# Two queues for the first loads of a gated attention and feed-forward mix, and new orders for its five engines

## The chip, the cores and the metric

The kernel runs on one core of one Trainium2 chip. The metric is the device time of one execution in microseconds (us); lower is better. A core has five engines that run their own instruction streams and meet through semaphores: TensorE (matrix products; PE in the profile, and PEld for its weight loads), VectorE (DVE), ScalarE (ACT), GpSimd (POOL) and SyncE (SP), which here only issues transfers. Matrix products read SBUF and write PSUM, which has 8 banks of 128 x 512 floats. SyncE and ScalarE can each issue transfers (DMAs) on a queue of its own; the profile calls these queues SPq and ACTq.

## The reference

```python
def _A_ref(x, wqkv, w_phi, wo):          # x: 1 x 2048 x 512, 32 heads of 16
    q, k, v = split(x @ wqkv)
    pq = einsum("bhsd,hdf->bhsf", q, w_phi)
    pk = einsum("bhsd,hdf->bhsf", k, w_phi)
    phi_q = concatenate([softmax(pq), softmax(-pq)])
    phi_k = concatenate([softmax(pk), softmax(-pk)])
    kv = einsum("bhsf,bhsd->bhfd", phi_k, v)
    z = einsum("bhsf->bhf", phi_k)
    num = einsum("bhqf,bhfd->bhqd", phi_q, kv)
    den = einsum("bhqf,bhf->bhq", phi_q, z)[..., None] + 1e-6
    return merge_heads(num / den) @ wo
def _B_ref(x, w1, w2):                   # w1: 512 x 1376, w2: 1376 x 512
    return maximum(x @ w1, 0) @ w2
g = sigmoid((x * gate_w).sum(-1, keepdims=True))
out = g * _A_ref(...) + (1 - g) * _B_ref(...)
```

Inputs and output are bf16.

## The kernel before

The 2048 rows of x form 16 tiles of 128 rows (m = 0 to 15), and 4 chunks of 512 rows (c = 0 to 3). Most products want x transposed, in SBUF tile XT. Chunks 1 to 3 are transposed by the transfer that loads them (tasks x1, x2, x3). The first four tiles are loaded as they are, into a free slot of FT, and turned on TensorE by a product with the identity IDN: tasks xt0a to xt3b (line 321), two 128-column matmuls each, tile m in halves a and b. ScalarE copies half a of a turned tile out of PSUM (xe00, xe10, xe20, xe30; line 333), VectorE half b (xe01 to xe31; line 335). The table XB says which PSUM banks each turned tile uses; with XB = (0,1), (6,7), (0,1), (6,7), tile 2 has to wait until tile 0 was copied out of banks 0 and 1.

The program is a set of small named tasks, each with its engine and the tasks that it depends on. A table ORDER holds, for each engine, the order in which its tasks are emitted; the waits are placed from the dependencies. Every engine does its tasks strictly in that order. The numbers `dur` and `lat` in the code are notes of the planner that made the orders; nothing emitted depends on them.

The tasks that matter below:

- warm0 (line 251): eight products of constants on TensorE, which keep it at work while the first load is under way; 3,456 columns in all.
- xa, wva, xb, wvb, w1a, wphi, wkT (lines 264 and 268): the first loads, all on SyncE's queue in this order. xa has tiles 0 to 2 of x (384 KB, three rows in each partition), xb tile 3 (128 KB), wva and wvb the two halves of the value weights (256 KB each), w1a 512 columns of w1 (512 KB); wkT is a transposing load of the key weights.
- v0a, v0b, ... v3a, v3b (line 369): the value product of tiles 0 to 3 in two halves, of two matmuls each; half a needs xe{m}0 and wva, half b xe{m}1 and wvb. ve0 to ve3 copy the results out on ScalarE (line 374). v4 to v15 are whole.
- h{c}_{k} (line 392), rl{c}_{k} (line 410): the first feed-forward layer, four matmuls a task, and its relu on ScalarE. The last 96 columns of the layer and the gate are hr{c} (line 400) and rr{c} (line 415), with a transposing transfer ht{c} (line 421).
- f1_j (line 351): folds w_phi into the key weights; fe1_j (lines 313, 315) copies the result out. It needs wkT and the block-diagonal w_phi (wbd, line 305).
- jobs k0 to k8 and q0 to q8, one or two tiles each: pr (line 449) projects, ev (line 482) copies out on ScalarE, mx and mn (lines 486, 488) are maximum and minimum on VectorE, t1 and t2 (line 495) the two subtractions on GpSimd, ex (line 500) the exponential on ScalarE, sm and rc (lines 502, 506) the sums and their reciprocals on VectorE, nm (lines 509 and 532) the division on GpSimd. For k, kv (line 516) sums key features times values over all tiles in PSUM; for q, ra (line 528) prepares the factor, tq{m} (line 535) transposes the features by a transfer on SyncE's queue, nd{m}_0 and nd{m}_1 (line 559) are numerator and denominator, rd and o (lines 565, 567) divide, and to{m} (line 572) transposes the result, again on SyncE's queue.
- b{m} (line 580, 11 matmuls) is the second feed-forward layer, a{m} (line 586, 4 matmuls) the output projection added in the same bank, oe{m} (line 631) the eviction on ScalarE, st{m} (line 634) the store, issued by ScalarE. Tile 15 is done in two column parts (lines 601, 612), so that its two stores go out from ScalarE and SyncE.
- ones (line 242): a memset on GpSimd that writes the column of ones into VS, from which z comes.

Of the kernel before, what the change touches and what calls it, by code (L numbers as in the profile page):

```python
# [15 lines left out]

ORDER = {
    "sp": (
        "xa wva xb wvb w1a wphi wkT w1b x1 gw w1c wqT x2 x3 w2a ht0 w2b ht1 wo ht3 tq0 tq1 tq3 tq2 to0 to1 tq4 "
        "tq5 to2 to3 tq6 tq7 to4 ht2 to5 tq9 tq8 to6 to7 tq10 tq11 to8 to9 tq12 tq13 to10 to11 tq14 tq15 to12 "  # L20
        "to13 to14 to15 st15_1 "
    ),
    "pool": (
# [5 lines left out]
    ),  # L29
    "act": (  # L30
# [8 lines left out]
    ),  # L39
    "dve": (  # L40
# [10 lines left out]
    ),  # L51
# [10 lines left out]
    ),  # L62
}

# [16 lines left out]
class _Graph:  # L81
# [6 lines left out]
    def add(self, name, eng, fn, deps=(), dur=0.1, lat=None, dma=False):  # L88
        assert name not in self.tasks, name
        found = []  # L90
        for d in deps:
            if d is None:
                continue
            t = self.tasks[d]
            if t not in found:
                found.append(t)
        self.tasks[name] = _Task(name, eng, fn, found, dur, self.LAT[eng] if lat is None else lat, dma)
        return name
# [44 lines left out]
def bass_gated_mix__linear_kernel_hedgehog__dense_activation_relu__prompt_kernel(  # L143
# [11 lines left out]
    x2 = A_x.rearrange("b s d -> (b s) d")  # L155
    o2 = out.rearrange("b s d -> (b s) d")
    S, D = x2.shape
# [23 lines left out]
    with ExitStack() as es:  # L181
# [67 lines left out]
        def pe_warm(q, sizes):  # L249
            for n in sizes:  # L250
                last = q.matmul(PS[:, 5, 0:n], ONE[:, 0:P], ONE[:, 0:n], start=True, stop=True)  # L251
            return last

        add("warm0", "pe", lambda q: pe_warm(q, (D, D, D, D, D, D, P, 2 * P)), (), dur=1.46)

        queue = {}

# [5 lines left out]
        def load(name, eng, out_, in_, deps=(), dur=0.1, lat=6.0, **how):  # L263
            add(name, eng, lambda q: q.dma_start(out=out_, in_=in_, **how), deps, dur=dur, lat=lat, dma=True)
            after_last(name, eng)
# [7 lines left out]

        w1r = B_w1.rearrange("(j p) n -> p j n", p=P)
        wvr = A_wqkv[:, 2 * D:3 * D].rearrange("(j p) n -> p j n", p=P)
        load("xa", "sp", FT[:, NF - 2, 0:3 * D], x2[0:3 * P, :].rearrange("(p t) d -> p (t d)", t=3), dur=0.47, lat=2.6)
        load("wva", "sp", WV[:, 0:2, :], wvr[:, 0:2, :], dur=0.47, lat=3.3)
        load("xb", "sp", FT[:, NF - 2, 3 * D:4 * D], x2[3 * P:4 * P, :], dur=0.47, lat=4.2)
        load("wvb", "sp", WV[:, 2:4, :], wvr[:, 2:4, :], dur=0.49, lat=3.8)
        load("w1a", "sp", W1[:, :, 0:512], w1r[:, :, 0:512], dur=0.5, lat=4.9)  # L280
        load("wphi", "sp", WPS[:, :, :], A_w_phi.rearrange("(g hl) r c -> (hl r) g c", g=ND), dur=0.55, lat=4.7)
        load_t("wkT", WT[:, ND:2 * ND, :], A_wqkv[:, D:2 * D], (), 4.55, 2.0)
# [31 lines left out]
            else:  # L314
                add(name, eng, lambda q: q.tensor_copy(out_, PS[:, b, :]), deps, dur=0.69)

        XB, FB = ((0, 1), (6, 7), (0, 1), (6, 7)), (6, 7, 0, 1)

        def pe_xt(q, m, n):
            for j in (2 * n, 2 * n + 1):  # L320
# [4 lines left out]
        for m in range(4):  # L325
            for n in range(2):
                add(f"xt{m}{'ab'[n]}", "pe", lambda q, m=m, n=n: pe_xt(q, m, n),
                    ("xa" if m < 3 else "xb", "ident", f"xe{m - 2}{n}" if m > 1 else None), dur=0.11)
            for n, eng in enumerate(("act", "dve")):
                xo = XT[:, 2 * n:2 * n + 2, m * P:(m + 1) * P]  # L330
                xi = PS[:, XB[m][n], 0:2 * P].rearrange("p (j t) -> p j t", j=2)
                if eng == "act":
                    add(f"xe{m}{n}", eng, lambda q, o=xo, i=xi: q.activation(o, i, ACT.Copy), (f"xt{m}a",), dur=0.38)
                else:
                    add(f"xe{m}{n}", eng, lambda q, o=xo, i=xi: q.tensor_copy(o, i), (f"xt{m}b",), dur=0.42)
# [6 lines left out]
        HB = (3, 4, 5)  # L342

        def rows(m):
            if m < 3:
                return o2[0:3 * P, :].rearrange("(p t) d -> p t d", t=3)[:, m, :]
            return o2[m * P:(m + 1) * P, :]

        def pe_fold(q, s, j, b):
            for i in range(ND):  # L350
                last = q.matmul(PS[:, b, i * P:(i + 1) * P], WT[:, s * ND + i, j * P:(j + 1) * P], WBD[:, i, :],  # L351
                                start=True, stop=True)
            return last

        for j in range(ND):
            b = FB[j]
            add(f"f1_{j}", "pe", lambda q, j=j, b=b: pe_fold(q, 1, j, b), ("wkT", *wbd, f"xe{3 - j // 2}{j % 2}"), dur=0.24)
            evict(f"fe1_{j}", ("dve", "act")[j % 2], WP[:, 1, j, :], b, (f"f1_{j}",))
        units = []
        for c in range(NC):  # L360
# [17 lines left out]
        for m in range(4):  # L378
            for n, js in enumerate(((0, 1), (2, 3))):
                add(f"v{m}{'ab'[n]}", "pe", lambda q, m=m, js=js: pe_v(q, m, js, VB[m]),  # L380
                    (f"xe{m}{n}", f"wv{'ab'[n]}", *((f"v{m}a",) if n else ())), dur=0.44)
            evict_v(m, VB[m], (f"v{m}b",))
        freed = {b: (f"ve{m}",) for m, b in enumerate(VB)}
        add("gt", "pe", lambda q: q.matmul(PS[:, 2, 0:ND], GWR[:, :], IDN[:, 0:ND], start=True, stop=True),
# [297 lines left out]
```

## Time and profile before

| | us |
|---|---|
| median of 3 runs | 150.82 (150.82 to 150.91) |
| the profiled execution | 150.61 |
| its span, first to last instruction | 148.8 |

| engine | busy us | share of the span |
|---|---|---|
| PE | 145.4 | 98% |
| DVE | 110.9 | 75% |
| POOL | 109.7 | 74% |
| ACT | 91.8 | 62% |
| PEld | 73.1 | 49% |

A row of the timeline has the start, the length, the engine, the line of the kernel, the operation and its operands (out<-in), the count (x) where like instructions are merged, and in brackets how long the engine had been idle and what ended that. Rows of the waits give the engine and what it waited for, then the total, the times and the longest. In the chain that ended last, each row is a start, a length and the work that the end of the execution hung on at that time. Matmuls are pipelined: a 512-column one is shown 379 ns long, while four of them take 0.86 us.

### The profile page before, as it was taken

To read this page: it belongs to the slowest core of one execution; us is meant where nothing else is said; L and a number is where in the kernel's file an instruction comes from. 1 tells how busy PE (TensorE), PEld (TensorE's weight loads), DVE (VectorE), ACT (ScalarE), POOL (GpSimd) and SP (SyncE) were. 2 spreads that over 40 slices of the span, in tenths; PEclk is the share of its full clock that TensorE was granted. 3 is DMA by queue.
4 is the path that set the end of the run, shared out by engine and by line. 5 is a ranking of instruction groups with operands and counts; after the bars stand their busy time and mean duration, and the time that the engine had idled before them with its cause. 6 is when DMAs were issued, how large, how long until landed. Compare 5 with 4: busy or idle time off the path is not lost.

```text
span 148.8 us, 2554 instructions
## 1 busy us (share of the span) xinstructions
PE 145.4 (98%) x984; PEld 73.1 (49%) x984; DVE 110.9 (75%) x169; ACT 91.8 (62%) x127; POOL 109.7 (74%) x73
## 2 busy tenths in 40 slices
PE   7999999999999999999999999999999999999994
PEld 2454444445446644455455544454545445445453
DVE  0345799999997769893979979799899966618301
ACT  3367779996795987865988691656545651303051
POOL 4000899999999999999999999999999924510000
PEclk9999999999999999999999999999999999999999
DMA  4999999300200500000000135964737587874543
GB/s 164 289 224 185 261 206 289 109 0 0 66 0 0 154 31 0 0 0 0 4 2 0 35 87 127 108 152 95 181 71 176 151 206 142 162 160 116 127 141 110
DMA packets 45524, 16.11 MB, mean 108 GB/s; under 512 B 39272, under 2 KB 45384, under 8 KB 45512
## 3 DMA queue, kind: packets, MB, share of 16 engines
q1 hardware_dynamic: 43208, 13.89, 42.9%
q10 hardware_dynamic: 2304, 2.06, 4.3%
q8 instruction: 8, 0.13, 0.4%
q14 instruction: 4, 0.03, 0.1%
HBM read 4.41 MB, written 2.10 MB: 44 GB/s over the span
## 4 chain that ended last, share of the span: by engine, by line
POOL 46%; PE 42%; issue 5%; DMA 3%; DVE 1%; SPq 1%; ACT 1%
POOL TS L495 25%; PE PS L580 19%; POOL FT L509 18%; PE PS L586 9%; DMA PHQ<-FT 3%; POOL FT L532 3%; PE PS L559 3%; PE PS L369 2%; PE PS L251 2%; PE PS L449 2%; PE PS L392 2%; PE PS L601 2%; SPq L535 1%; PE PS L321 1%; PE PS L351 1%
## 5 line engine op out<-in xcount | busy, mean ns | idle before, releaser
L495 POOL TENSOR_TENSOR TS<-MN,PB 128x1024 bf16<-128x1024 bf16 (+1 forms) x18 | 31.0, 1733 | 12.9 <-DVE MN L488 12.9
L392 PE MATMUL PS<-XT,W 128*128 128x512 bf16 x160 | 38.4, 379 | 0.0
L502 DVE TENSOR_REDUCE ZB<-FT 128x128 f32<-128x2048 bf16 (+1 forms) x18 | 36.4, 2029 | 1.9 <-ACT FT L500 1.8
L580 PE MATMUL PS<-W,HT 128*128 128x512 bf16 (+1 forms) x165 | 37.8, 379 | 0.0
L500 ACT ACTIVATE FT<-TS 128x2048 bf16<-128x2048 bf16 (+1 forms) x18 | 30.9, 1719 | 4.3 <-POOL TS L495 3.6
L495 POOL TENSOR_TENSOR TS<-PB,MX 128x1024 bf16<-128x1024 bf16 (+1 forms) x18 | 31.1, 1732 | 0.0
L449 PE MATMUL PS<-WP,XT 128*128 128x512 bf16 x128 | 30.1, 379 | 0.0
L509 POOL TENSOR_TENSOR FT<-FT,SC 128x2048 bf16<-128x2048 bf16 (+1 forms) x9 | 29.7, 3308 | 0.0
L631 ACT ACTIVATE OSB<-PS,OMG 128x512 bf16<-128x512 f32 x15 | 10.3, 686 | 24.9 <-PE PS L586 24.8
L410 ACT ACTIVATE HT<-PS 128x512 bf16<-128x512 f32 x40 | 22.6, 596 | 4.7 <-PE PS L392 3.9
L580 PEld LDWEIGHTS PS<-W,HT 128*128 128x128 bf16 (+1 forms) x165 | 15.4, 98 | 17.2 <-ACT OSB L631 0.7
L482 ACT ACTIVATE PB<-PS 128x1024 bf16<-128x1024 f32 (+1 forms) x18 | 16.7, 928 | 10.7 <-PE PS L449 5.7
L392 PEld LDWEIGHTS PS<-XT,W 128*128 128x128 bf16 x160 | 14.7, 98 | 16.4 <-ACT HT L410 0.9
L488 DVE TENSOR_REDUCE MN<-PB 128x64 bf16<-128x1024 bf16 (+1 forms) x18 | 19.4, 1090 | 4.4 <-ACT PB L482 4.3
L486 DVE TENSOR_REDUCE MX<-PB 128x64 bf16<-128x1024 bf16 (+1 forms) x18 | 19.4, 1086 | 3.6 <-ACT PB L482 3.6
L449 PEld LDWEIGHTS PS<-WP,XT 128*128 128x128 bf16 x128 | 12.2, 98 | 14.2 <-ACT PB L482 0.5
L369 PE MATMUL PS<-WV,XT 128*128 128x512 bf16 x64 | 16.4, 379 | 0.1
L532 POOL TENSOR_TENSOR FT<-FT,SR 128x1024 bf16<-128x1024 bf16 (+1 forms) x9 | 15.7, 1740 | 0.6
L586 PE MATMUL PS<-WO,OT 128*128 128x512 bf16 x60 | 14.8, 378 | 0.0
L567 DVE SCALAR_TENSOR_TENSOR OTM<-PS,EG,RD 128x256 bf16<-128x256 f32 x32 | 14.3, 468 | 0.2
L565 DVE RECIPROCAL RD<-PS 128x16 f32<-128x16 f32 x32 | 6.7, 235 | 9.0 <-PE PS L559 9.0
L374 ACT ACTIVATE VS<-PS 128x512 bf16<-128x512 f32 x16 | 9.4, 600 | 2.2 <-PE PS L369 2.2
(54 smaller groups left out, 97.5 us busy)
## 6 DMA issues: line engine op xcount, KB each, us to landing
out_dram<-OSB ACTq DMA_DIRECT2D x15, 128.0 KB, 2.0
W<-in_B_w_dram SPq DMA_DIRECT2D x1, 1280.0 KB, 7.4
W<-in_B_w_dram SPq DMA_DIRECT2D x2, 512.0 KB, 4.9
WV<-in_A_wqkv_dram SPq DMA_DIRECT2D x2, 256.0 KB, 3.7
WO<-in_A_wo_dram SPq DMA_DIRECT2D x1, 512.0 KB, 3.8
FT<-in_A_x_dram SPq DMA_DIRECT2D x1, 384.0 KB, 3.0
W<-in_B_w_dram SPq DMA_DIRECT2D x1, 352.0 KB, 3.6
PHQ<-FT SPq DMA_TRANSPOSE x16, 2.8
```

What stands on the lines that cost most here:

```text
L392: last = q.matmul(PS[:, b, :], W1[:, j, k * P:(k + 1) * P], XT[:, j, chunk(c)], start=(j == 0), stop=(j == ND - 1))
L410: add(f"rl{a}_{k}", "act", lambda q, a=a, k=k, b=b: q.activation(HT[:, k, chunk(a)], PS[:, b, :], ACT.Relu), (f"h{a}_{k}",), dur=0.6)
L449: last = q.matmul(PS[:, pj + n, :], XT[:, j, m * P:(m + 1) * P], WP[:, s, j, :], start=(j == 2), stop=(j == 1))
L486: add(f"mx_{J}", "dve", lambda q, sl=sl, w=w, i=pbg: q.tensor_reduce(MX[:, sl, 0:w * H], i, AX.X, ALU.max), (f"ev_{J}", old("t1")), dur=0. ...
L488: add(f"mn_{J}", "dve", lambda q, sl=sl, w=w, i=pbg: q.tensor_reduce(MN[:, sl, 0:w * H], i, AX.X, ALU.min), (f"ev_{J}", old("t2")), dur=0. ...
L495: add(f"{tn}_{J}", "pool", lambda q, o3=o3, a3=a3, b3=b3: q.tensor_tensor(o3, a3, b3, ALU.subtract), (f"{'mx' if sg == 0 else 'mn'}_{J}", ...
L500: add(f"ex_{J}", "act", lambda q, fs=fs, ts=ts, w=w: q.activation(FT[:, fs, 0:w * F], TS[:, ts, 0:w * F], ACT.Exp), (f"t1_{J}", f"t2_{J}", ...
L502: add(f"sm_{J}", "dve", lambda q, fs=fs, sl=sl, w=w: q.tensor_reduce(ZB[:, sl, 0:2 * w * H], FT[:, fs, 0:w * F].rearrange("p (g d) -> p g ...
L509: add(f"nm_{J}", "pool", lambda q, f3=f3, sl=sl, w=w: q.tensor_tensor(f3, f3, SC[:, sl, 0:2 * w * H].unsqueeze(2).to_broadcast([P, 2 * w * ...
L532: add(f"nm_{J}", "pool", lambda q, f3=f3, r3=r3: q.tensor_tensor(f3, f3, r3, ALU.mult), (f"ra_{J}",), dur=0.19 + 0.86 * w)
L580: last = q.matmul(PS[:, ab, :], HT[0:r, k, m * P:(m + 1) * P], W2[0:r, k, :], start=(k == 0), stop=False)
L586: last = q.matmul(PS[:, ab, :], OT[:, m % NOT, t, :], WO[:, t, :], start=False, stop=(t == ND - 1))
```

## The change

Three things are changed.

The first loads. SyncE issues two loads of two tiles each, xa0 (tiles 0 and 1) and xa1 (tiles 2 and 3), 256 KB each, two rows in each partition; ScalarE issues wva and wvb on its own queue, as its first two instructions. w1a, wphi, wkT and all later ones follow on SyncE's queue. Since rows lie in partitions by pairs now, the store of tiles 0 to 3 goes back the same way (`rows`).

The warming's last product has 128 columns instead of 256.

The orders of all five engines are new, with the banks that go with them: turned tile 2 uses banks 4 and 5, turned tile 3 banks 0 and 1. So tile 2 no longer waits for tile 0's copies, tile 3 does, and v3, whose result goes to bank 5, waits for xe21.

```diff
-        add("warm0", "pe", lambda q: pe_warm(q, (D, D, D, D, D, D, P, 2 * P)), (), dur=1.46)
+        add("warm0", "pe", lambda q: pe_warm(q, (D, D, D, D, D, D, P, P)), (), dur=1.41)
...
-        load("xa", "sp", FT[:, NF - 2, 0:3 * D], x2[0:3 * P, :].rearrange("(p t) d -> p (t d)", t=3), dur=0.47, lat=2.6)
-        load("wva", "sp", WV[:, 0:2, :], wvr[:, 0:2, :], dur=0.47, lat=3.3)
-        load("xb", "sp", FT[:, NF - 2, 3 * D:4 * D], x2[3 * P:4 * P, :], dur=0.47, lat=4.2)
-        load("wvb", "sp", WV[:, 2:4, :], wvr[:, 2:4, :], dur=0.49, lat=3.8)
+        def pair(i):
+            return x2[2 * i * P:2 * (i + 1) * P, :].rearrange("(p t) d -> p (t d)", t=2)
+
+        load("xa0", "sp", FT[:, NF - 2, 0:2 * D], pair(0), dur=0.47, lat=2.5)
+        load("wva", "act", WV[:, 0:2, :], wvr[:, 0:2, :], dur=0.47, lat=3.2)
+        load("xa1", "sp", FT[:, NF - 2, 2 * D:4 * D], pair(1), dur=0.47, lat=3.45)
+        load("wvb", "act", WV[:, 2:4, :], wvr[:, 2:4, :], dur=0.47, lat=4.2)
...
-        XB, FB = ((0, 1), (6, 7), (0, 1), (6, 7)), (6, 7, 0, 1)
+        XB, FB = ((0, 1), (6, 7), (4, 5), (0, 1)), (6, 7, 0, 1)
...
-                    ("xa" if m < 3 else "xb", "ident", f"xe{m - 2}{n}" if m > 1 else None), dur=0.11)
+                    (f"xa{m // 2}", "ident", f"xe0{n}" if m > 2 else None), dur=0.11)
...
-                    (f"xe{m}{n}", f"wv{'ab'[n]}", *((f"v{m}a",) if n else ())), dur=0.44)
+                    (f"xe{m}{n}", f"wv{'ab'[n]}", f"v{m}a" if n else "xe21" if m == 3 else None), dur=0.44)
```

Parts of the orders, for the places that the prediction speaks of:

```diff
 sp, from the start and around the first tq
-xa wva xb wvb w1a wphi wkT w1b x1 gw w1c wqT x2 x3 w2a ht0 w2b ht1 wo ht3 tq0 tq1 tq3 tq2 to0 to1 tq4 tq5
+xa0 xa1 w1a wphi wkT w1b x1 gw w1c wqT x2 x3 w2a ht0 w2b ht1 wo ht2 tq0 tq1 tq2 tq3 to0 to1 tq5 tq4
 pool, from the start
-iota_r iota_i iota_c gwz pads ones t2_k0 t1_k0 t1_k1 t2_k1
+iota_r iota_i iota_c gwz pads t2_k0 ones t1_k0 t1_k1 t2_k1
 act, from the start
-xe00 xe10 xe20 xe30 ve2 ve0 ve1 ve3 fe1_3 rl0_1 fe1_1 rl0_0 ev_k0 rl0_2 ev_k1
+wva wvb xe00 xe10 xe20 xe30 ve2 ve1 rl0_1 fe1_3 fe1_1 ve3 ev_k0 ev_k1 rl0_0 rl0_2 ve0
 dve, around the first job
-fe1_2 fe1_0 mx_k0 mn_k0 mx_k1 mn_k1
+fe1_2 fe1_0 mn_k0 mx_k0 mx_k1 mn_k1
 pe, from the start
-warm0 xt0a xt0b xt1a xt1b xt2a xt2b v0a v2a v1a xt3a v1b v2b xt3b v0b v3a h0_1 v3b h0_0 f1_3 f1_2 f1_0 f1_1 h0_2 pr_k0a pr_k0 pr_k1 pr_k2
+warm0 xt0a xt0b xt1a xt1b v0a xt2a xt2b v1a xt3a v2a v2b xt3b v1b v3a h0_1 h0_0 f1_3 f1_2 f1_0 f1_1 v3b v0b pr_k0a pr_k0 pr_k1 h0_2 pr_k2
 pe, around the first nd
-b2 h3_8 kv15 b1 nd0_0 nd0_1 pr_q6 nd1_0 nd1_1 b0 nd2_0 pr_q7 a0 nd3_0 nd2_1 a1 nd3_1 b3
+b2 h3_8 kv15 b1 nd0_0 nd1_0 nd0_1 pr_q6 nd1_1 b0 nd2_1 nd2_0 pr_q7 a0 nd3_0 nd3_1 a1 b3
 act, the end
-oe12 st10 st7 oe13 st12 oe14 st9 st14 st13 oe15_0 st15_0
+oe12 st12 oe14 oe13 st14 st10 st13 oe15_0 st15_0
```

More of the change, by code (lines that the diff above doesn't have):

```diff
@@ L18 @@
     "sp": (
-        "xa wva xb wvb w1a wphi wkT w1b x1 gw w1c wqT x2 x3 w2a ht0 w2b ht1 wo ht3 tq0 tq1 tq3 tq2 to0 to1 tq4 "
-        "tq5 to2 to3 tq6 tq7 to4 ht2 to5 tq9 tq8 to6 to7 tq10 tq11 to8 to9 tq12 tq13 to10 to11 tq14 tq15 to12 "
-        "to13 to14 to15 st15_1 "
+        "xa0 xa1 w1a wphi wkT w1b x1 gw w1c wqT x2 x3 w2a ht0 w2b ht1 wo ht2 tq0 tq1 tq2 tq3 to0 to1 tq5 tq4 to2 "
+        "to3 tq6 tq7 to4 ht3 to5 tq8 tq9 to6 to7 tq11 tq10 to8 to9 tq12 tq13 to10 tq14 to11 tq15 to12 to13 to14 "
+        "to15 st15_1 "
     ),
     "pool": (
[1 row of a table removed]
[1 row of a table added]
         "t1_k4 t2_k5 t1_k5 nm_k2 t1_k6 t2_k7 t2_k6 t1_k7 nm_k3 nm_k4 t1_k8 t2_k8 t2_q0 nm_k5 t1_q0 nm_k6 t2_q1 "
[3 rows of a table removed]
[3 rows of a table added]
     ),
     "act": (
[8 rows of a table removed]
[8 rows of a table added]
     ),
     "dve": (
[2 rows of a table removed]
[2 rows of a table added]
         "rc_k3 sm_k4 mx_k7 mn_k6 mn_k7 rc_k4 fe0_0 gr1 fe0_3 fe0_2 fe0_1 sm_k5 mn_k8 mx_q0 mn_q0 mx_k8 sm_k6 "
[7 rows of a table removed]
[7 rows of a table added]
     ),
     "pe": (
[2 rows of a table removed]
[2 rows of a table added]
         "v5 h1_3 pr_k6 h1_4 kv0 v6 hr0 pr_k7 h1_2 h1_7 h1_6 h1_5 v7 kv1 h1_8 pr_k8 h1_9 v8 hr1 f0_0 kv2 v9 f0_2 "
         "f0_1 f0_3 kv3 v10 kv4 h2_2 h2_0 pr_q0 h2_3 h2_5 pr_q1 v11 kv5 h2_1 kv6 h2_6 pr_q2 v12 h2_8 h2_4 kv7 "
[5 rows of a table removed]
[5 rows of a table added]
     ),
@@ L344, in rows @@
         def rows(m):
-            if m < 3:
-                return o2[0:3 * P, :].rearrange("(p t) d -> p t d", t=3)[:, m, :]
+            if m < 4:
+                i = m // 2
+                return o2[2 * i * P:2 * (i + 1) * P, :].rearrange("(p t) d -> p t d", t=2)[:, m % 2, :]
             return o2[m * P:(m + 1) * P, :]
@@ L356, in bass_gated_mix__linear_kernel_hedgehog__dense_activation_relu__prompt_kernel @@
             b = FB[j]
-            add(f"f1_{j}", "pe", lambda q, j=j, b=b: pe_fold(q, 1, j, b), ("wkT", *wbd, f"xe{3 - j // 2}{j % 2}"), dur=0.24)
+            add(f"f1_{j}", "pe", lambda q, j=j, b=b: pe_fold(q, 1, j, b), ("wkT", *wbd, f"xe{(1, 3)[j // 2]}{j % 2}"), dur=0.24)
             evict(f"fe1_{j}", ("dve", "act")[j % 2], WP[:, 1, j, :], b, (f"f1_{j}",))
```

56 rows, old and new, of the table ORDER are left out of this document.

## The prediction

> **What bounds the kernel now.** I read busy time by stretch first (a row is the stretch, its length, busy time and count of TensorE's matmuls, its weight loads, VectorE, ScalarE and GpSimd, TensorE's clock, the DMA share and GB/s), then the opening engine by engine, then the chain that ended last.
>
> ```profile
> 3.80:8.40 4.60, 4.39 (x31) 2.23 (x32) 1.83 (x6) 2.23 (x6) 0.00 (x0) 1.00 1.09 271
> 8.40:95.80 87.40, 87.40 (x604) 44.37 (x603) 73.87 (x85) 67.10 (x94) 80.26 (x41) 1.00 0.37 77
> ...
> 96.36:146.60 50.24, 50.23 (x342) 25.48 (x342) 33.97 (x78) 20.36 (x28) 27.07 (x23) 1.00 0.61 143
> 146.60:148.80 2.20, 0.00 (x0) 0.00 (x0) 0.38 (x1) 0.31 (x1) 0.00 (x0) 1.00 0.34 107
> ```
>
> TensorE is the bound: from 8.40 to 95.80 and from 96.36 to 146.60 it is busy throughout. New orders can win nothing inside these stretches; they can only open holes. What can be won lies before 8.40, in the short piece at 96, and in the last 2.20 us, whose two stores the change leaves alone.
>
> The opening:
>
> ```profile
> 0.78 3.01 PE L251 MATMUL PS<-const-bfloat16-1.0 128*128 128x512 bf16 x8 [0.78 <-PEq L667]
> 3.81 0.45 PEld L321 LDWEIGHTS PS<-IDN,FT 128*128 128x128 bf16 x8 [0.37 <-DMA FT<-in_A_x_dram]
> 4.57 0.27 PEld L321 LDWEIGHTS PS<-IDN,FT 128*128 128x128 bf16 x4 [0.31 <-ACT XT L333]
> ...
> 6.54 1.02 PE L369 MATMUL PS<-WV,XT 128*128 128x512 bf16 x4
> 8.38 1.03 PE L392 MATMUL PS<-XT,W 128*128 128x512 bf16 x4
> ```
>
> Warming ends before x lands; the first turn (xt0a) starts at 3.81; xt2a waits 0.31 for ScalarE to empty a bank (4.57); v1b starts at 6.54, after its weights. The loads behind this, the queue's start times and then time to landing of x (2 loads), of the value weights (2), of w1a and of the transpose wkT:
>
> ```profile
> 0.74 0.41 SPq L264 DMA_DIRECT2D FT<-in_A_x_dram  x1
> 1.20 0.42 SPq L264 DMA_DIRECT2D WV<-in_A_wqkv_dram  x1
> 1.67 0.46 SPq L264 DMA_DIRECT2D FT<-in_A_x_dram  x1
> 2.17 0.43 SPq L264 DMA_DIRECT2D WV<-in_A_wqkv_dram  x1
> 2.65 0.47 SPq L264 DMA_DIRECT2D W<-in_B_w_dram  x1
> 3.71 4.10 SPq L268 DMA_TRANSPOSE WT<-in_A_wqkv_dram  x1
> ...
> DMA to landing us min/median/max: 3.0/3.3/3.6
> ...
> DMA to landing us min/median/max: 3.2/3.7/4.2
> ...
> DMA to landing us min/median/max: 5.2/5.2/5.2
> ...
> DMA to landing us min/median/max: 6.2/6.2/6.2
> ```
>
> So xa (384 KB) lands at 0.74 + 3.0 = 3.74, wva (256) at 4.40, xb (128) at 5.27, wvb (256) at 6.37, w1a (512) at 7.85, wkT at 9.91. By bytes asked for in order: 384 KB at 3.74, 640 at 4.40, 768 at 5.27, 1024 at 6.37, 1536 at 7.85. The transfers, not their issue, set these times:
>
> ```profile
> 2.40:3.40 1.00, 1.00 (x5) 0.41 (x3) 0.00 (x0) 0.00 (x0) 0.08 (x1) 1.00 1.00 376
> 3.80:4.50 0.70, 0.62 (x8) 0.45 (x8) 0.25 (x1) 0.36 (x2) 0.00 (x0) 1.00 0.96 240
> ...
> 5.30:6.40 1.10, 1.10 (x7) 0.51 (x6) 0.18 (x1) 0.00 (x0) 0.00 (x0) 1.00 1.03 355
> ```
>
> From 2.40 on the DMA share (second to last column) is about 1. The middle, from the chain that ended last:
>
> ```profile
> 7.56 0.11 PE PS L321 x2
> ...
> 11.59 0.86 PE PS L392 x4
> ...
> 90.62 1.23 SPq L535
> ...
> 91.90 4.41 DMA PHQ<-FT
> ...
> 96.35 0.30 PE PS L559 x4
> ```
>
> and, from TensorE's timeline, the start of b0, the work ahead of nd2_0:
>
> ```profile
> 93.66 2.54 PE L580 MATMUL PS<-W,HT 128*128 128x512 bf16 x11
> ```
>
> When nm_q1 is done on GpSimd, SyncE issues tq3 (90.62, 1.23 us) and only behind it, at 91.90, tq2, which nd2_0 waits for. Four matmuls of 512 columns take 0.86, so b0's eleven take 2.37 and are through at 96.03; nd2_0 starts at 96.35: a hole of 0.32.
>
> **The change, part by part.** The warming loses 128 columns, 0.11 us at 3.01 us for 3,456 columns; it already ends before the x load, which hides it (without that cover it would be a gain of 0.11 at most).
>
> *The loads.* xa0 and xa1 (256 KB each) go out at 0.74 and 1.20, w1a at about 1.67 and wkT at about 2.75, 0.95 earlier (two issues of about 0.47 fewer on SyncE). wva and wvb leave on ScalarE's queue at about 0.74 and 1.20; ScalarE's table load waits behind them:
>
> ```profile
> 0.73 1.28 ACT L333 ACT_TABLE_LOAD   x1 [0.73 <-PEq L667]
> 4.13 1.14 ACT L333 ACTIVATE XT<-PS 128x256 bf16<-128x256 f32 x3 [2.12 <-PE PS L321]
> ```
>
> It would end at 0.74 + 0.92 + 1.28 = 2.94; the first eviction comes at 4.13, so 1.2 us of idle ScalarE hide it; with an issue twice as long it would still be hidden.
>
> To cost the opening I take the start of h0_1, 8.38. Before it run the 16 turns and seven half products; in the new order the same turns and six (v0b and v3b follow). A half product (two matmuls) is 0.43, a pair of turns 0.11, so a draw is 7.95. From xt2a on the new order has xt2 0.22, v1a 0.43, xt3a 0.11, v2 0.86, xt3b 0.11, v1b 0.43, v3a 0.43, together 2.59; from v2b on 1.40. Three times gate it. First, v0a now waits for the same ScalarE eviction, 0.76 after the first turn, so xt2a cannot start before 3.81 + 0.76 + 0.43 = 5.00 (h0_1 at 7.59, a gain of 0.36). Second, xa1 must have landed: h0_1 is its landing + 0.07 (as 3.74 to 3.81) + 2.59, a draw at 5.29. Third, wvb: landing + 0.17 (as 6.37 to 6.54) + 1.40, a draw at 6.38. Bytes being the bound, xa0, wva, xa1, wvb in this order put xa1 at the 768 KB mark, 5.27, and wvb at 1024 KB, 6.37: a draw to 0.02. w1a (7.85) and then wkT must be there as well; f1, 0.86 earlier in the order than before, comes at 7.95 + 1.73 = 9.68 and needs wkT, at 9.91 by bytes or 8.96 if its issue sets it: a wait of 0 to 0.23. I take 0, since its issue of 4.10 us is the long part of its 6.2. Bounds of the opening: from a gain of 0.36 to a loss of 0.73 (third rival).
>
> By the Trainium skill, page DMA: Bandwidth & Descriptors, section Issuing engines are not separate DMA queues, transfers started by several engines run interleaved on the same 16 engines and save only issue time. The share of 1 above fits it; no run so far shows two loading queues together. By it the earlier issue of wva and wvb wins nothing and their packets mix with the others', which is the third rival's time.
>
> *The start of GpSimd's chain.* pr_k0 now comes ahead of h0_2, 0.86 earlier, and the minimum ahead of the maximum.
>
> ```profile
> 1.81 0.67 POOL L242 MEMSET VS<- 128x128 bf16 x1
> ...
> 14.67 0.60 DVE MN L488
> ...
> 15.35 2.06 POOL TS L495 x2
> ```
>
> t2_k0 can start when the first reduction is done, and the memset of ones (0.67, once in an idle engine) fills the 0.60 until t1_k0: a cost of 0.07 against 0.86. GpSimd's chain, and with it nm_q1, should come 0 to 0.8 earlier.
>
> *The middle.* tq2 takes tq3's place. The transposes issued there took 4.41 us to their use, which is 95.03 from 90.62; TensorE needs tq2 at 96.03. The hole of 0.32 closes. Next are a0 and a1, behind to0 and to1:
>
> ```profile
> 94.53 2.58 SPq L572 DMA_TRANSPOSE OT<-OTM  x2
> 98.47 1.02 PE L586 MATMUL PS<-WO,OT 128*128 128x512 bf16 x4
> ...
> DMA to landing us min/median/max: 2.4/2.4/2.4
> ```
>
> The second goes out at about 95.82 and lands at 98.22; a1 would start at 98.47 - 0.32 = 98.15. If the queue is not earlier at all, 0.1 of the 0.32 returns; with nm_q1 earlier, none. I take 0.32, with 0.2 as the lower bound; nothing in the middle offers more than the hole.
>
> On SyncE's queue ht2 and ht3 trade places, ht2 now ahead of tq0; it waits for rr2, which ScalarE's new order has before rr3, so tq0 is not held up longer than behind ht3.
>
> *The remaining orders* cost nothing where TensorE was full. ScalarE's last run is longer: two evictions of 0.69 and three stores of 0.36 (2.5 us) under b15 and a15_0, whose 22 and 8 matmuls take 3.30:
>
> ```profile
> L631 ACT ACTIVATE OSB<-PS,OMG 128x512 bf16<-128x512 f32 x15 | 10.3, 686 | 24.9 <-PE PS L586 24.8
> ...
> 143.31 2.41 PE PS L601 x22
> 145.72 0.89 PE PS L612 x8
> 146.94 0.36 ACTq L625 DMA_DIRECT2D out_dram<-OSB  x1
> ```
>
> Without that cover the last eviction would be late by the part that sticks out.
>
> **Sum.** Opening 0.02, middle 0.32, rest 0: 0.34. The profiled execution took 150.61 for a span of 148.8; the median is 150.82, 0.21 above. Span 148.46, profiled time 150.27, median 150.48.
>
> **Rivals.** *Loads really come earlier* (the issue counts): xa1 by 4.9, wvb by 6.0, w1a by 7.5; the opening gains its 0.36 instead of 0.02: 150.14. For it: 376 GB/s were reached for a while, and 240 and 355 later. Against: a share of 1.
>
> *The middle wait moves on*, to a1: if tq3, to0 and to1 are each as much later behind tq2 as TensorE is earlier, the 0.32 returns, 150.80. For: a1 already starts only 0.25 after to1 lands (98.47 against 98.22); against: GpSimd's earlier start.
>
> *The second queue gets in the way (slower).* wvb on ScalarE's queue shares each DMA engine with xa1 and then w1a. If they alternate, wvb ends when 256 KB of w1a have passed too: 1280 KB, half way between 6.37 and 7.85, 7.11. h0_1 is then at 8.68, a loss of 0.73; with the middle's gain 150.82 + 0.73 - 0.32 = 151.23. It is slower than before from a wvb landing at 6.70, and by more than 0.3 from 7.00. For it: the full DMA share. Against: wva and wvb are issued early, so half of w1a need not lie ahead of wvb.
>
> *The clock stays low.* The warming's 3,456 columns take 3.01 us, later 2,048 take 0.86: half the rate, until about 3.8. If the shorter warming missed the rise for another 3.0 us, about 1.2 would be lost: 151.7. The Trainium skill, TensorE: Matmul & The Clock Gate, Part 1, has the clock follow a free-running activity window; the trace shows the rise, not the window.
>
> **Chances.** Forecast 0.45 (150.25 to 150.70), earlier loads 0.14, moved wait 0.15, second queue 0.22, clock 0.04. About 0.2% (0.30 us) is what a measurement tells from no change: faster means under 150.52. The forecast lies close to that edge: of its 0.45 I count 0.29 as faster and 0.16 as the same; earlier loads add 0.14 to faster; moved wait 0.14 to same, 0.01 to slower; the second queue 0.02, 0.07 and 0.13; the clock 0.04 to slower. Faster 0.45, same 0.37, slower 0.18. The range, 150.0 to 151.2, holds all but the ends of the first and the last two rivals.
>
> **What would show it.** Right: h0_1 at about 7.95 and TensorE waiting about 0.3 for xa1 at 5.0; no hole before nd2; t2_k0 near 14. Wrong: wvb after 6.7, a hole ahead of f1 or h0_1, turns of 0.1 us each (clock), a hole at a1, or a new one of over 0.3 anywhere after 8.

## The result, and the profile after

| | before | after |
|---|---|---|
| median of 10 runs each, us | 150.79 (150.34 to 151.72) | 151.48 (150.91 to 151.81) |
| ratio after / before, 95% interval | | 1.0043 (1.0025 to 1.0061) |
| the profiled execution, us | 150.61 | 151.50 |
| its span, us | 148.8 | 150.0 |
| time outside the span, us | 1.81 | 1.50 |

The changed kernel is slower, by 0.65 us as the ratio has it. Ratios, here and below, leave out executions more than 1.5% above their kernel's fastest, which the medians include; of a_swap below that takes four of twelve.

Its busy time by stretch of TensorE (columns as in the prediction):

```profile
3.80:8.25 4.45, 3.77 (x28) 2.13 (x29) 1.81 (x6) 2.20 (x6) 0.00 (x0) 1.00 1.16 327
8.25:135.42 127.17, 126.27 (x860) 64.29 (x875) 105.64 (x154) 84.00 (x115) 108.19 (x64) 1.00 0.49 98
135.42:136.74 1.32, 0.19 (x6) 0.06 (x3) 1.17 (x4) 0.74 (x2) 0.00 (x0) 1.00 1.11 312
...
147.80:150.00 2.20, 0.00 (x1) 0.00 (x0) 0.38 (x1) 0.32 (x1) 0.00 (x0) 1.00 0.20 60
```

Before, the stretch from 8.40 on had one hole, of 0.32 at 96. After, that one is gone, and there is one at 135.42. (The 0.90 missing from the second row is no hole: this trace has 966 of 984 matmul records, and a matmul of 512 columns that is not recorded leaves a gap of about 0.2.) The stretch behind TensorE's last matmul is 2.20 us as before.

TensorE's timeline at the new hole:

```profile
135.19 0.42 PE L563 MATMUL PS<-KVN,PHQ 128*128 128x68 bf16 x8
136.74 2.55 PE L584 MATMUL PS<-W,HT 128*128 128x512 bf16 x11 [1.13 <-ACT OSB L635]
```

Where nothing holds TensorE up, eight such matmuls make room for the next task 0.26 after their start (133.05 and 133.31 in the trace of before). So b13 could have started at 135.45 and started at 136.74, 1.29 later; the row has 1.13 because it counts from the modelled end of the last matmul. The text below calls this hole 1.30. The chain that ended last goes through it:

```profile
129.87 0.88 PE PS L590 x4
...
130.78 0.70 ACT OSB L635
...
131.49 0.34 ACTq L638
...
131.87 0.45 ACTq L638
...
132.35 3.57 DMA out_dram<-OSB
...
136.00 0.70 ACT OSB L635
...
136.74 2.55 PE PS L584 x11
```

Read upwards: b13 (136.74) waits for a PSUM bank that oe10 empties (136.00); oe10 waits for the landing of a store that was issued at 132.35 and landed 3.57 us later. ScalarE's timeline there:

```profile
130.78 0.69 ACT L635 ACTIVATE OSB<-PS,OMG 128x512 bf16<-128x512 f32 x1 [2.71 <-PE PS L590]
131.49 2.51 ACTq L638 DMA_DIRECT2D out_dram<-OSB  x5
136.00 0.69 ACT L635 ACTIVATE OSB<-PS,OMG 128x512 bf16<-128x512 f32 x1 [4.54 <-DMA out_dram<-OSB]
```

The evictions write into eight buffers of OSB in turn, so oe10 needs the one that oe2 filled and st2 must first have emptied. The new order of ScalarE has "oe9 st9 st6 st2 st3 st5 oe10": st2, whose data has been there since oe2 was through at 106.3, is the third of five stores issued in a row, one eviction ahead of the task that needs its buffer. Before, st2 went out 18 us ahead of that task; ScalarE's timeline, and the answer on OSB around that store:

```profile
116.59 0.34 ACTq L634 DMA_DIRECT2D out_dram<-OSB  x1
...
134.37 0.69 ACT L631 ACTIVATE OSB<-PS,OMG 128x512 bf16<-128x512 f32 x1 [5.01 <-PE PS L586]
```

```profile
DMA to landing us min/median/max: 1.7/1.7/1.7
```

There oe10 (134.37) waits for TensorE alone. That store, alone, landed 1.7 us after its issue began; the third of five in a row took 3.57.

The opening after, on TensorE, and the times from issue to landing of xa0 and xa1, then of wva and wvb:

```profile
4.34 0.72 PE L324 MATMUL PS<-IDN,FT 128*128 128x128 bf16 x8 [0.64 <-DMA FT<-in_A_x_dram]
5.20 0.61 PE L373 MATMUL PS<-WV,XT 128*128 128x512 bf16 x2
5.64 0.39 PE L324 MATMUL PS<-IDN,FT 128*128 128x128 bf16 x4
...
8.25 1.46 PE L396 MATMUL PS<-XT,W 128*128 128x512 bf16 x6
```

```profile
DMA to landing us min/median/max: 3.6/4.0/4.4
```

```profile
DMA to landing us min/median/max: 4.1/4.6/5.1
```

The issues of xa0 and wva begin at 0.74, those of xa1 and wvb at 1.22 and 1.24, so these four land at about 4.3, 4.9, 5.6 and 6.3. TensorE idles 0.64 for xa0. With 8.25 for h0_1 the opening is 0.30 later than a draw (7.95). The profile's difference of 1.2 us in span is then 0.30 for the opening, -0.32 in the middle and 1.30 for the new hole, 1.28 in all; 0.31 comes back outside the span, where no row shows it. (Between the two profiled executions that leaves a loss of 0.89; by the ratio of all of them it is 0.65.)

### The profile page after: what moved, and what is told of

It reads as the page before. It is cut to its first block, busy times and chain, and to the rows that moved or that the text cites. A ratio compares the mean times of both kernels' runs of the same rounds, so it can differ in the third digit from the quotient of the medians.

```text
span 150.0 us, 2538 instructions
## 1 busy us (share of the span) xinstructions
PE 144.2 (96%) x966; PEld 73.6 (49%) x984; DVE 110.5 (74%) x169; ACT 91.3 (61%) x127; POOL 109.4 (73%) x73
## 3 DMA queue, kind: packets, MB, share of 16 engines
HBM read 4.41 MB, written 2.10 MB: 43 GB/s over the span
## 4 chain that ended last, share of the span: by engine, by line
PE 77%; ACT 7%; POOL 5%; DMA 5%; issue 3%; DVE 1%; ACTq 1%
PE PS L584 22%; PE PS L396 17%; PE PS L453 14%; PE PS L373 7%; PE PS L590 7%; POOL TS L499 5%; PE PS L520 3%; DMA out_dram<-OSB 2%; DMA FT<-in_A_x_dram 2%; ACT PB L486 2%; PE PS L563 2%; PE PS L605 2%; ACT HT L414 1%; PE PS L404 1%; ACT FT L504 1%
## 5 line engine op out<-in xcount | busy, mean ns | idle before, releaser
L584 PE MATMUL PS<-W,HT 128*128 128x512 bf16 (+1 forms) x158 | 36.9, 379 | 1.5 <-ACT OSB L635 1.1
L373 PE MATMUL PS<-WV,XT 128*128 128x512 bf16 x61 | 15.8, 379 | 0.3
```

Of the source, the lines that this page charges most:

```text
L373: last = q.matmul(PS[:, b, :], XT[:, j, m * P:(m + 1) * P], WV[:, j, :], start=(j == 0), stop=(j == ND - 1))
L584: last = q.matmul(PS[:, ab, :], HT[0:r, k, m * P:(m + 1) * P], W2[0:r, k, :], start=(k == 0), stop=False)
```

## The experiments

Every kernel was compared with the kernel before on the same chip. "Outside" is the median, over a kernel's runs, of its time less its span; for the kernel before it was 1.86 to 1.88 in the three batches that had many runs.

| kernel | median us (before there) | ratio (95%) | median span (before there) | outside |
|---|---|---|---|---|
| a_store | 150.36 (151.06) | 0.9955 (0.9935 to 0.9975) | 148.8 (149.2) | 1.54 |
| a_sp | 152.89 (151.06) | 1.0128 (1.0079 to 1.0178) | 151.05 (149.2) | 1.87 |
| a_both | 151.12 (151.06) | 1.0001 (0.9982 to 1.0020) | 149.25 (149.2) | 1.84 |
| b_act | 150.49 (151.06) | 0.9973 (0.9953 to 0.9993) | 149.0 (149.2) | 1.52 |
| a_dose | 149.79 (150.49) | 0.9956 (0.9939 to 0.9973) | 148.35 (148.6) | 1.46 |
| b_tq | 150.51 (150.49) | 0.9991 (0.9976 to 1.0006) | 148.7 (148.6) | 1.83 |
| a_warm | 150.02 (150.49) | 0.9968 (0.9952 to 0.9984) | 148.65 (148.6) | 1.41 |
| b_wphi | 150.76 (151.03) | 0.9984 (0.9964 to 1.0005) | 149.0 (149.1) | 1.74 |
| a_tab | 150.01 (151.03) | 0.9936 (0.9911 to 0.9962) | 148.5 (149.1) | 1.54 |
| a_swap | 152.49 (151.03) | 1.0040 (0.9998 to 1.0081) | 151.05 (149.1) | 1.54 |
| b_best | 150.31 (151.03) | 0.9982 (0.9948 to 1.0016) | 148.9 (149.1) | 1.43 |

**First batch: the stores or the loads?** a_store is the changed kernel with st2 and st3 moved forward:

```diff
-st0 gp2 oe6 oe7 ev_q8 gp3 st1 st7 oe8 ex_q8 oe9 st9 st6 st2 st3 st5 oe10
+st0 st2 gp2 oe6 oe7 ev_q8 gp3 st1 st7 st3 oe8 ex_q8 oe9 st9 st6 st5 oe10
```

> The changed kernel with two stores moved earlier in ScalarE's order (st2 behind st0, st3 behind st7), nothing else. Theory STORE (the late hole of 1.3 us on TensorE at 135 is oe10 waiting for the landing of st2, issued only 4 us before; it is most of the loss): the hole goes, the span falls from 150.0 to about 148.9, the time to about 150.7, level with before, while h0_1 stays at 8.25. Theory LOADS (the loss is the opening, where loads on two queues land later): the hole is refilled by another wait, and the time stays over 151.2.

a_sp is the changed kernel with all its loads on SyncE:

```diff
-sp: xa0 xa1 w1a    act: wva wvb xe00
+sp: xa0 wva xa1 wvb w1a    act: xe00
```

> The changed kernel with all four first loads issued by SyncE, in the order xa0, wva, xa1, wvb; ScalarE issues none of them. STORE: the opening recovers 0.3 us or so, the hole at 135 stays, about 151.2. LOADS: the first turn comes at 3.8 or earlier, h0_1 at about 7.9, and the time falls to 150.9 or less.

a_both has both edits.

> Both edits: stores moved earlier and all first loads by SyncE. If the two losses add, 1.2 and 0.3 of the profiled span come back: span about 148.5, time about 150.4, faster than before by the middle hole of 0.32. If STORE alone explains the loss, the same as the kernel with moved stores alone; if LOADS alone, the same as the kernel with the loads on SyncE alone.

b_act is the kernel before with one edit, its value weights issued by ScalarE:

```diff
-sp: xa wva xb wvb w1a    act: xe00
+sp: xa xb w1a    act: wva wvb xe00
```

> The kernel before, its orders and its loads of three tiles and one, but wva and wvb issued by ScalarE. LOADS: the first loads start slower on two queues, xa lands at about 4.3 instead of 3.74 and the opening loses 0.3 to 0.6: about 151.2. STORE: nothing in its late part changes, so it stays at 150.8.

With st2 and st3 moved, the hole is gone: ScalarE's timeline of a_store has st2 behind st0 (114.68, x2), and ahead of oe10 (now 133.49) there is only the issue of three other stores.

```profile
114.68 1.08 ACTq L638 DMA_DIRECT2D out_dram<-OSB  x2
...
133.49 0.69 ACT L635 ACTIVATE OSB<-PS,OMG 128x512 bf16<-128x512 f32 x1 [1.76 <-issue]
```

TensorE in a_store, over the stretch of the hole:

```profile
134.00:137.50 3.50, 3.50 (x28) 1.82 (x27) 1.91 (x6) 0.86 (x2) 0.00 (x0) 1.00 1.10 233
```

The kernel that had been slower becomes faster than the kernel before, 0.9955. The loads, put back on SyncE, made it worse instead of better, with the hole (a_sp) as without it (a_both); neither theory had foretold that. a_both's TensorE shows where: it waits for xa1, and then for w1a (h0_1 at 8.79) and for wkT (f1 at 10.87), which go out later than in a_store, behind more loads in one queue, and which the new order needs sooner than the old.

```profile
5.49 0.40 PE L324 MATMUL PS<-IDN,FT 128*128 128x128 bf16 x4 [0.47 <-DMA FT<-in_A_x_dram]
...
8.79 1.89 PE L396 MATMUL PS<-XT,W 128*128 128x512 bf16 x8 [0.52 <-DMA W<-in_B_w_dram]
10.87 1.07 PE L355 MATMUL PS<-WBD,WT 128*128 128x128 bf16 x16 [0.20 <-DMA WT<-in_A_wqkv_dram]
```

The queue alone doesn't explain w1a: before, behind as many bytes in one queue and issued at the same 2.65, it landed after 5.2 us, here after 6.0, and why is open. In a_sp's profile xa1 holds TensorE up by 0.63, the clock stays low until about 6.5 (read from the matmuls: 512 columns take 0.43 at the low clock and 0.22 later), and the late hole is 1.44 long where after has 1.13.

So in this kernel the loads on two queues are a gain over the loads on one: a_store against a_both is 0.46%, 0.69 us; by the medians the spans differ by 0.45 and the outside by 0.30. In b_act, where only the queues differ from before, the median span is 0.2 shorter and the outside 0.34. Its one profile doesn't show an earlier opening as the reason: the first turn comes at 4.18 and h0_1 at 9.15, 0.37 and 0.77 later than in before's, and the low clock lasts to about 6.3.

**Second batch: which part of the five stores, and the other terms.** a_dose keeps the five stores in a row and only exchanges their places:

```diff
-oe9 st9 st6 st2 st3 st5 oe10
+oe9 st2 st3 st9 st6 st5 oe10
```

> The changed kernel with the same five stores in the same place behind oe9, but st2 and st3 first among them instead of third and fourth (st2, st3, st9, st6, st5), so st2 goes out about 0.85 us earlier. STORE (oe10 waits for the landing of st2): the hole on TensorE shrinks from 1.3 us to 0.5 or less, and the time falls by 0.6 to 1.1 us from the changed kernel's, to about 150.6. Rival ISSUE (the five issues in a row, 2.5 us, keep ScalarE from the eviction): hole and time stay, about 151.5.

b_tq is the kernel before with tq2 ahead of tq3.

```diff
-tq0 tq1 tq3 tq2 to0
+tq0 tq1 tq2 tq3 to0
```

> The kernel before with tq2 and tq3 exchanged in SyncE's order, nothing else. If the middle hole of 0.32 us was tq2 standing behind tq3, it closes and the time falls by 0.2 to 0.32 us, ratio about 0.998; if the transposes were late for another reason, the hole stays at nd2 or moves to nd3 or a1, ratio 1.000.

a_warm is a_store with 512 more columns of warming.

```diff
-pe_warm(q, (D, D, D, D, D, D, P, P))
+pe_warm(q, (D, D, D, D, D, D, D, P, P))
```

> The changed kernel with the two stores moved, and with 512 more columns of warming (0.43 us at the low clock), up to about 3.9, which ends before xa0 lands at 4.1 to 4.3. If the pause of 0.6 us ahead of the first turn makes the clock rise late, it rises by the first turn now and the time falls by 0.3 to 0.7 us to about 149.9; if the moment of the rise is a matter of chance in each execution, nothing changes, 150.36 within 0.2, and the turns may again start at 0.107 us each.

b_again is the kernel before, unchanged, for a second profile of it.

> The kernel before once more, for a second profile, on the chip of the other kernels. If the moment of the clock's rise is a matter of chance, the turns and value products of this execution may start at the low clock (107 and 427 ns apart) although the first profile had them at 56 and 216; landings of the first loads within 0.3 us of the first profile's. If the clock follows the warming, the rise comes at about 3.7 again.

ScalarE's timeline of a_dose:

```profile
130.28 3.03 ACTq L638 DMA_DIRECT2D out_dram<-OSB  x5
133.42 0.69 ACT L635 ACTIVATE OSB<-PS,OMG 128x512 bf16<-128x512 f32 x1 [2.45 <-issue]
134.90 0.69 ACT L635 ACTIVATE OSB<-PS,OMG 128x512 bf16<-128x512 f32 x1 [0.79 <-PE PS L590]
```

The five issues still stand ahead of oe10 and even take longer (3.03 against 2.51), yet oe10 starts at 133.42 and the hole is gone. The store that is issued first, at 130.28, now is st2:

```profile
DMA to landing us min/median/max: 1.8/1.8/1.8
```

It is 1.57 earlier against the start of oe9 than in the changed kernel, nearly twice the 0.85 that was expected, since it does not wait for oe9 as st9 did; and it lands in 1.8 instead of 3.57. So oe10 waits for the issues (2.45 <-issue) and no longer for the landing, and TensorE doesn't wait for oe10. So it was neither the number of stores nor ScalarE's time to issue them, but the late landing of the one store whose buffer is needed next. Both a_store and a_dose move st3 along with st2; that it is st2 that holds oe10 up is read from the chain above. From 1.0043 to 0.9956 is 0.87%, 1.31 us; each ratio has about 0.18% on either side, so that this fits the hole's 1.30, and the last digit is chance.

b_tq shows no difference that could be told from none, though there is no hole at nd2 in its profile. b_again shows that this profile proves nothing of the exchange. Its window around nd2, the starts of h0_1 and of b0 on TensorE, and the issues and landings of tq3 and tq2:

```profile
95.80:96.40 0.60, 0.60 (x8) 0.29 (x6) 0.60 (x1) 0.60 (x1) 0.60 (x1) 1.00 0.65 143
```

```profile
8.65 1.03 PE L392 MATMUL PS<-XT,W 128*128 128x512 bf16 x4
...
93.92 2.54 PE L580 MATMUL PS<-W,HT 128*128 128x512 bf16 x11
```

```profile
L535 SPq DMA_TRANSPOSE PHQ<-FT x2: 1232/1654/2077, 90.9 to 92.2; - x2
DMA to landing us min/median/max: 3.9/4.1/4.2
```

In this execution of the very same kernel TensorE reaches h0_1 0.27 later (by the matmuls' spacing the low clock lasts to about 5.8), and nd2 doesn't wait at all. The span is 148.7, against 148.8. TensorE reaches b0 0.26 later too (93.92 against 93.66), and SyncE issues the two transposes 0.27 later (90.9 against 90.62): the chain moves with the opening. What differs is the landing. tq2, issued at 92.2, lands 3.9 us later, at 96.1, where in the first profile it took 4.41 and came at 96.31; b0 is through at 96.3. With 3.9 the first execution would have had tq2 at 95.8, ahead of the 96.03 at which b0 was through there. So the hole of 0.32 is, by these two executions, a matter of how long one transpose takes to land, and it is not in every execution of the kernel before.

a_warm gained nothing over a_store (0.9968 and 0.9955, in different batches), and in its profile the clock rose later than in most, at about 6.0.

**Third batch: the time outside the span.** Kernels whose ScalarE issues two of the four first loads (512 KB) have 1.4 to 1.54 us outside the span, those whose SyncE issues all of them 1.83 to 1.88. b_wphi, the kernel before with only wphi (16 KB) issued by ScalarE, asks whether the first transfer of ScalarE's queue does it; a_tab is a_dose with a small activation ahead of wva (on ones, into a buffer that is overwritten later), to ask whether it matters that the table load comes first; a_swap is a_dose with wva on SyncE and xa1 on ScalarE; b_best is b_act with b_tq's order.

```diff
 b_wphi
-sp: wvb w1a wphi wkT    act: xe00
+sp: wvb w1a wkT    act: wphi xe00
 a_tab
+add("tab", "act", lambda q: q.activation(OSB[:, 0, :], ONE[:, :], ACT.Copy), (), dur=0.6)
 a_swap
-sp: xa0 xa1 w1a    act: wva wvb xe00
+sp: xa0 wva w1a    act: xa1 wvb xe00
 b_best
-sp: xa wva xb wvb w1a ... tq3 tq2    act: xe00
+sp: xa xb w1a ... tq2 tq3    act: wva wvb xe00
```

> The kernel before with one small load, wphi (16 KB), issued by ScalarE as its first instruction instead of by SyncE; wva and wvb stay on SyncE's queue. Every kernel so far whose ScalarE begins with loads has 1.30 to 1.61 us of measured time outside its span, every other one 1.78 to 2.02. Theory FIRST (what ScalarE does first, a table load or a transfer, sets that part): outside falls to about 1.5, time by about 0.36. Rival BULK (it falls because the 512 KB of value weights are off SyncE's queue): outside stays at 1.87; span within 0.3 of before either way.

> The changed kernel with st2 and st3 first among the five stores, and a copy of constants into an unused buffer as ScalarE's first instruction, so that the table load comes first again and wva and wvb go out about 1.9 us later, still from ScalarE. FIRST: outside rises back to about 1.87. BULK: outside stays at about 1.5. Span: wvb lands some 1.5 us later, 7.3 or so, so h0_1 waits for it and the span is 0.5 to 1.3 us longer than 148.35.

> The changed kernel with st2 and st3 first among the five stores, and the first loads crossed: SyncE issues xa0 and wva, ScalarE xa1 and wvb. If the opening is set by xa1's landing (5.07 to 5.57 so far), xa1 now lands by 4.5, wva by 5.2, and the opening gains up to 0.2 us: 0.9945 of before. If wva's landing sets it instead (v0a is ahead of xt2a in the order), it loses 0.2 to 0.4: 0.998.

> The kernel before, its orders, with two parts of the change alone: wva and wvb issued by ScalarE, and tq2 ahead of tq3. If the two parts add, 0.997 (queues) and 0.999 (tq) give 0.996, level with the changed kernel after its stores are mended; if the new orders have a worth of their own, this one stays behind at 0.997 to 0.998.

b_wphi has 1.74, a third of the way, with 16 KB of 512. a_tab did not do what it was made for: ScalarE's timeline has its table load first, but the transfers' issue does not wait for it.

```profile
0.74 1.28 ACT L256 ACT_TABLE_LOAD   x1 [0.74 <-PEq L673]
0.81 0.97 ACTq L266 DMA_DIRECT2D WV<-in_A_wqkv_dram  x2
```

So it says only that the order of the table load and the first issue is not the cause (1.54 still), and that this order does no harm: 0.9936 is the best ratio of all, though the intervals of a_tab, a_dose and a_store overlap. b_best, 0.9982, is not told apart from b_act or from no change. Three of its twelve executions lie at 151.74 to 152.31 and nine at 150.11 to 150.69; the ratio takes in all twelve, so it doesn't settle whether the two parts add. What makes the outside shorter stays open. It is shorter wherever ScalarE takes over first loads, but not in proportion to their bytes, and whether one transfer against two makes the difference, nothing here tells.

a_swap's executions fall in two groups, four with spans of 149.0 to 149.6 and eight with 150.8 to 151.4, and its ratio of 1.0040 mixes the two. Its profile is one of the second group:

```profile
5.58 1.01 PE L373 MATMUL PS<-WV,XT 128*128 128x512 bf16 x2 [0.41 <-DMA WV<-in_A_wqkv_dram]
...
7.88 1.87 PE L373 MATMUL PS<-WV,XT 128*128 128x512 bf16 x4
...
9.69 1.03 PE L373 MATMUL PS<-WV,XT 128*128 128x512 bf16 x4
10.56 1.68 PE L396 MATMUL PS<-XT,W 128*128 128x512 bf16 x7
```

Four value matmuls take 1.87 at 7.88 and 1.03 at 9.69: the clock stayed low until about 9.6, and h0_1 comes at 10.56 where a_dose has 7.75. The part of it that belongs to the crossed loads is the wait of 0.41 for wva: xa1 landed at about 4.3, and wva's landing set the opening, the second of the two cases that were expected.

## Why the prediction was wrong, step by step

**"The remaining orders cost nothing where TensorE was full": this step failed.** It was more than the whole error. The prediction itself had said that new orders can only open holes in these stretches, then looked for one at a1, at ht2 and at ScalarE's last run, and set the rest at 0 without following any ring of buffers. A new hole of over 0.3 anywhere after 8 was among its own signs of being wrong, and that is what came. ScalarE's order in the change has it in plain sight: st2 behind oe9, oe10 behind it, eight buffers. In the rows of before oe10 stands 18 us behind st2, and the change leaves less than one landing between them. It cost 1.30, shown by a_store and a_dose, which take it away by moving st2 and its neighbour st3 forward. With 1.30 added, the sum of 0.34 gained becomes 0.96 lost, 151.78; measured was 0.65 lost. The 0.31 between them can't be given to one term: 0.31 was gained outside the span, which the sum did not have, the opening of the profile came 0.32 worse than the sum had it, and the middle's 0.32 is not there in every execution.

**The middle, 0.32: the wait was there in the row, but not in every execution.** After, nothing separates b0 from the two nd tasks behind it; the chain that ended last has

```profile
94.10 2.32 PE PS L584 x10
96.43 0.26 PE PS L563 x8
```

and neither f1 nor a1 waits. In a_dose, whose opening is earlier still (7.75), TensorE doesn't wait there either. But the size was read from one execution. b_again has no such hole with the old order, since its transposes land sooner. b_tq, which changes that order alone, gives 0.9991 (0.9976 to 1.0006), 0.14 us, and its interval goes from 0.36 gained to 0.09 lost: what the exchange is worth on the average is not settled.

**The start of GpSimd's chain: right.** t2_k0 was said to start near 14 and the chain to be 0 to 0.8 earlier:

```profile
14.20 1.05 POOL L499 TENSOR_TENSOR TS<-MN,PB 128x512 bf16<-128x512 bf16 x1 [12.33 <-DVE MN L492]
```

Before, it was 15.35. SyncE's first tq comes at 86.16 against 86.44, 0.28 earlier; the memset cost nothing visible.

**The opening, 0.02: the gates fit, the landings were rough.** The second gate gives h0_1 as the landing of xa1 + 2.66: 5.57 + 2.66 = 8.23, measured 8.25. In a_dose, xa1 lands at 5.07 and h0_1 starts at 7.75 (formula 7.73), a gain of 0.20 where after's profile has a loss of 0.30. But the first gate fits as well. The prediction had left its first turn at 3.81, as if xa0 landed when xa had; it came at 4.34 (a_dose 3.84). v0a follows the first turn by 0.86 (a_dose 0.87) and takes 0.43, and xt2a starts right behind it, at 5.64 (5.15). In both profiles the chain that ended last goes this way, from xa0's landing over the first eviction to v0a, and xa1 has just landed when it is through; these two traces can't tell which gate is the later. The bytes in order of issue, the prediction's 5.27 for xa1, lie between the two landings. What that estimate missed is that in both profiles the two queues moved less from 2.40 to 3.40 (298 and 255 GB/s against 376) and more from 3.80 to 4.50 (369 and 395 against 240); before's two rows for these times stand in the prediction. The first row here is before's, the next fence is after, the last a_dose:

```profile
1.80:2.40 0.60, 0.60 (x2) 0.15 (x1) 0.00 (x0) 0.22 (x1) 0.60 (x2) 1.00 0.68 164
```

```profile
1.80:2.40 0.60, 0.60 (x2) 0.15 (x1) 0.00 (x0) 0.60 (x1) 0.06 (x1) 1.00 0.72 55
2.40:3.40 1.00, 1.00 (x5) 0.42 (x3) 0.00 (x0) 0.64 (x1) 0.00 (x0) 1.00 0.88 298
...
3.80:4.50 0.70, 0.16 (x2) 0.17 (x3) 0.00 (x0) 0.00 (x0) 0.00 (x0) 1.00 1.04 369
```

```profile
1.80:2.40 0.60, 0.60 (x2) 0.15 (x1) 0.00 (x0) 0.60 (x1) 0.07 (x1) 1.00 0.81 205
2.40:3.40 1.00, 1.00 (x5) 0.41 (x3) 0.00 (x0) 0.65 (x1) 0.00 (x0) 1.00 0.83 255
...
3.80:4.50 0.70, 0.66 (x8) 0.62 (x8) 0.06 (x1) 0.23 (x1) 0.00 (x0) 1.00 1.06 395
```

Why the first 0.6 us differ so much between executions (55 and 205 GB/s) is open.

**ScalarE's last run: right.** It stayed covered; 2.20 us behind the last matmul, as before.

**The warming: right as far as it could be seen.** The shorter one, through at 3.70, still ends before xa0 lands.

**The rivals.** *The second queue gets in the way* named 151.23, near the time that came, for a reason that did not happen: wvb landed at 6.30, not behind 6.70, and by a_both and b_act two queues are a net gain. That nearness is luck. The Trainium skill, DMA: Bandwidth & Descriptors, Issuing engines are not separate DMA queues, says that several engines save only issue time, which is usually small. Here two issues fewer on SyncE let w1a go out at 1.67 (a_store) instead of 2.65 (a_both), 0.98 earlier, and a_store is 0.69 ahead, of which 0.30 lie outside the span. That the gain is issue time fits these numbers; in this kernel it is not small beside the 0.3 us that the change was about. The wait that was feared there came from DMA, but at the other end of the kernel, with a store. *Loads really come earlier*, 150.14, is what the change does without its store hole: a_dose's ratio of 0.9956 makes 150.16 out of 150.82, with xa1 at 5.07 and w1a at 7.40, though over half of that gain lies outside the span, where no rival had looked. a_store has the same ratio with h0_1 at 8.51 in its profile, later than before's, so that this match, too, is in good part luck. *The moved wait* did not come. *The clock stays low* named 151.7, as near as the second queue's 151.23. It did not come in the changed kernel's profile, where the turns are closer together from about 4.6 on (its spans are 149.4 to 150.4), but it is real: a_swap's profile has it, and eight of its twelve executions lie about 2 us higher, as that one does; that the clock is the reason in all eight is not shown. In the other kernels' profiles the spacing of the matmuls puts the rise between the first turn or sooner (before, a_tab) and some 6.7 us (b_wphi); a_warm, whose warming was the longest, has 6.0. The Trainium skill, TensorE: Matmul & The Clock Gate, Part 1, has the clock follow a free-running window; these moments agree with a rise that no instruction sets, and a_warm speaks against more warming as a remedy.

**The unit of account.** The prediction held the outside of the span fixed at 1.81. It fell by 0.3 to 0.47 in every kernel whose ScalarE issues two of the four first loads. That gain was in no row and could not be read from the profile of before.

## What to carry to other kernels

When an order is rewritten, walk each ring of buffers once: for every release that is moved (a store, a copy), find the next task that fills that buffer, and allow the landing time of a transfer in a queue of its like, not that of one alone. A stretch without holes deserves this more than the stretches with holes, since all it can do is lose. And before a hole is counted as gain, see in a second execution whether it is there at all: this one hung on a transpose that took 4.41 us to land in one execution and 3.9 in the next.

## What the runs showed of the hardware beside this

- Stores of 128 KB issued by ScalarE: one alone landed 1.7 us after its issue began, the first of five in a row after 1.8 (a_dose), the third of five after 3.57.
- The column of the granted clock reads 1.00 in every row shown, and it does where matmuls take double (a_swap until 9.6); in this case the low clock shows only in the matmuls' spacing.
- On ScalarE the issue of a transfer did not wait for a table load that began 0.07 us ahead of it and ran for 1.28 (a_tab).
